# Even and odd output rows, contiguous activation sums, one-bank tiles in the last pass and later fills in an attention-plus-FFN kernel

## The chip, the cores and the metric

One core of one Trainium2 chip. A time is the device time of one execution in microseconds (us); "span" is the time from the first to the last instruction in a profiled execution.

The profiles name the engines PE (TensorE matmuls), PEld (TensorE weight loads), DVE (VectorE), ACT (ScalarE), POOL (GpSimd) and SP (SyncE, which here issues most of the stores). A tile is a piece of memory that the program reserves and guards with waits; a bank is a piece of PSUM, the memory in which TensorE sums its products. A timeline merges instructions of one kind that follow each other into one line.

## The reference

```python
scores = where(mask, scale * q @ k.T, -1e9)      # (8, 8, 576, 64); heads 0-3: the last 32 positions,
attn   = softmax(scores) @ v                     # heads 4-7: positions with the same remainder mod 32
x   = attn.transpose(0, 2, 1, 3).reshape(4608, 512)
out = ((x @ w_a) * (x @ w_b)) @ w_out            # d_ff 1536, out (4608, 512) float32
```

The 4608 tokens are worked off in nine tiles of 512. Attention for later batches runs beside the FFN of earlier ones. In tiles 0 to 2 the product with `w_out` is a plain one; in tiles 3 to 8 ("fast tiles") it is a Strassen-like form with seven products over halves of the tokens, of d_ff and of d_model. Tile 8 is the last pass, in which nothing is left to run beside it.

## The kernel before

The parts that the change and the argument touch. `pf` holds `a * b`, transposed; `ps` holds five sums of its quarters; `wf` holds sums of quarters of `w_out`, `wo_sb` is `w_out` itself. `q` is one of two groups of 128 tokens, `i` a half of the tokens, `g` one of six slices of d_ff.

```python
    FG, HT, HN = FD // 2, TTOK // 2, d_model // 2          # 6, 256, 256
    # a_sb * ab[1] -> pf: token half i are alternate blocks of 16 rows
    halves = lambda x: x.rearrange("p (a i s) -> p a i s", i=2, s=16)
    nc.vector.tensor_mul(pf[:, f, :].rearrange("p (i a s) -> p a i s", i=2, s=16), halves(a_sb), halves(ab[1]))
    ...
    def fast_s(t, n, gs):                                  # the activation sums, on VectorE
        pss[t] = nat.tile([128, 5 * FD * TTOK // 4], ...).rearrange("p (g m) -> p g m", g=FG)
        s = pss[t][:, gs]                                  # g outermost, the five sums side by side in it
        ...
            nc.vector.tensor_tensor(s[:, :, HT:3 * HT]..., x[:, :, 0], x[:, :, 1], op=ALU.add)      # n == 1: sums 1 and 2
    ...
    # weights of the products: 128 neighbouring columns
    full   = lambda e, i: (lambda g, q: pf[:, 2 * g + e, HT * i + 128 * q:HT * i + 128 * (q + 1)])
    summed = lambda n: (lambda g, q: s[:, g, HT * n + 128 * q:HT * n + 128 * (q + 1)])
    ...
    def y_store(eng, t, y, i, q, n=slice(0, d_model)):     # 128 rows of the output
        rows = out[TTOK * t:TTOK * (t + 1), n].rearrange("(q a i s) c -> a s i q c", q=2, i=2, s=16)
        eng.dma_start(out=rows[:, :, i, q], in_=y[i][:, q, n])
    def store_half(i):                                     # fast tiles but the last
        for q in range(2):
            y_store(nc.sync, t, y, i, q)
    ...
    # y_tail, the last pass: for q in 0, 1: products 3 4 1 2 5 6 7 into banks a b c b a c d
        if q == 0:
            bank = {x: mm_bank([128, HN]) for x in "abcd"}
        else:
            o = psum4["o"].tile([128, 2, 512], F32, tag="o", name="end")
            st = pst.tile([128, 2, 512], F32, tag="st", name="end")
            bank = {"a": o[:, 0, :HN], "b": o[:, 1, :HN], "c": st[:, 0, :HN], "d": st[:, 1, :HN]}
    ...
    do(18, fill_v, vl_buf[1])                              # GpSimd: ones beside the values of batch 3
    do(19, fill_v, vs_buf[1])
```

The softmax here doesn't subtract the row's maximum and nothing guards it: scores larger than these inputs give would overflow.

## Time and profile before

| | before |
|---|---|
| time, median of 3 (range) | 337.25 us (336.41 to 339.04) |
| span of the profiled run, mean granted clock | 335.3 us, 0.998 |
| last pass: its first matmul to the end of the last VectorE operation | 318.83 to 330.67, 11.84 us |
| from there to the last byte stored | 2.55 us |
| last byte to the end of the span | 2.07 us |

### The profile page before, as it was taken

Reading aid. Unit: us, or ns where it says so; the run is one execution under the profiler, and the core shown is the slowest. Engines: PE = TensorE matmul, PEld = TensorE weight load, DVE = VectorE, ACT = ScalarE, POOL = GpSimd, SP = SyncE. Lnnn points to the kernel's source line nnn. Section 1 sums busy time; section 2 is a strip of 40 time slices with the busy share of each in tenths; the row PEclk is TensorE's granted clock in tenths of the full one; section 3 lists DMA queues with packets and bytes.
Section 4 is the critical chain, followed back from the end, with each engine's and each line's share of the span. In section 5 each row is a group of like instructions: output and inputs, shape, how many; then the busy total and the mean of one; then the engine's idle time right before and its main releaser. Section 6 shows DMA issues by size and latency. Waiting matters only on the chain.

```text
span 335.3 us, 7662 instructions
## 1 busy us (share of the span) xinstructions
PE 326.2 (97%) x2814; PEld 201.8 (60%) x2814; DVE 254.7 (76%) x489; ACT 202.8 (60%) x329; POOL 173.4 (52%) x295
## 2 busy tenths in 40 slices
PE   8999999999999999999999999999999999999992
PEld 6654555455555555556999885568556844674472
DVE  5867566768878985799999999999877845738641
ACT  5663955468678865776587757875788533223320
POOL 8945836499956644765577457754312031312011
PEclk9999999999999999999999999999999999999999
DMA  9999999599999599969888998899123021003013
GB/s 155 148 203 196 201 181 188 120 191 70 131 221 155 86 99 158 129 116 92 69 83 139 179 98 75 142 164 107 25 62 119 2 73 54 1 12 116 0 29 98
DMA packets 102173, 37.60 MB, mean 112 GB/s; under 512 B 77432, under 2 KB 97784, under 8 KB 102136
## 3 DMA queue, kind: packets, MB, share of 16 engines
q0 software_dynamic: 87760, 19.58, 64.4%
q1 hardware_dynamic: 14104, 17.34, 17.7%
q8 instruction: 22, 0.36, 0.4%
q10 hardware_dynamic: 272, 0.20, 0.2%
q14 instruction: 15, 0.12, 0.1%
HBM read 39.71 MB, written 9.44 MB: 147 GB/s over the span
## 4 chain that ended last, share of the span: by engine, by line
PE 75%; DMA 12%; POOL 7%; DVE 2%; issue 2%; ACT 0%; DVEq 0%; POOLq 0%
PE mm L545 44%; PE mm L650 14%; PE mm L730 7%; DMA vl<-in_v_dram 4%; PE o L454 4%; PE st L356 3%; DMA shared<-in_k_dram 3%; DMA wa_sb<-in_moe_w_a_dram 3%; PE end L678 1%; PE mm L678 1%; POOL shared L195 1%; DMA kl<-in_k_dram 1%; POOL ql L210 1%; DMA natk<-in_k_dram 1%; POOL vl L222 1%
## 5 line engine op out<-in xcount | busy, mean ns | idle before, releaser
L545 PE MATMUL mm<-xT,wb_sb 128*128 128x512 bf16 (+1 forms) x472 | 110.2, 357 | 0.1
L545 PE MATMUL mm<-xT,wa_sb 128*128 128x512 bf16 (+1 forms) x472 | 110.3, 358 | 0.0
L562 ACT COPY a_sb<-mm 128x512 f32<-128x512 f32 x106 | 62.2, 587 | 48.7 <-PE mm L545 46.4
L545 PEld LDWEIGHTS <-wb_sb 128*128 128x128 bf16 x480 | 46.4, 98 | 44.5 <-issue 0.6
L880 POOL CAST pace<-pf 1x1 f32<-1x1 bf16 x84 | 28.4, 339 | 85.1 <-DVE pf L565 73.8
L565 DVE TENSOR_TENSOR pf<-a_sb,mm 128x512 bf16<-128x512 f32 x72 | 48.5, 674 | 17.2 <-PE mm L545 13.8
L545 PEld LDWEIGHTS <-wa_sb 128*128 128x128 bf16 x480 | 42.6, 98 | 31.2
L364 ACT ACTIVATE p<-st 128x576 bf16<-128x576 f32 (+1 forms) x64 | 41.7, 651 | 9.5 <-PE st L356 9.0
L463 ACT ACTIVATE xr<-o 64x576 f32<-64x576 f32 x48 | 31.1, 648 | 26.1 <-PE o L454 25.9
L730 PE MATMUL mm<-wo_sb,pf 128*128 128x512 bf16 x144 | 34.4, 379 | 0.5 <-DMA wo_sb<-in_moe_w_out_dram 0.5
L464 ACT ACTIVATE xr<-xr 64x576 f32<-64x576 f32 x48 | 32.9, 685 | 1.5
L650 PEld LDWEIGHTS <-ps 128*128 128x128 bf16 x300 | 28.5, 98 | 4.4 <-DVE ps L578 1.2
L567 DVE TENSOR_TENSOR pf<-a_sb,mm 128x512 bf16<-128x512 f32 x34 | 23.0, 678 | 8.4 <-ACT a_sb L562 5.9
L470 DVE TENSOR_TENSOR xT<-o,xr 64x288 bf16<-64x288 f32 x48 | 21.5, 448 | 10.4 <-ACT xr L464 9.7
L468 DVE TENSOR_TENSOR xT<-o,xr 64x288 bf16<-64x288 f32 x48 | 21.5, 447 | 8.9 <-ACT xr L464 8.3
L374 DVE TENSOR_TENSOR p<-p,mask_l 128x576 int16<-128x576 int16 x32 | 19.8, 618 | 6.8 <-ACT p L364 6.7
L650 PE MATMUL mm<-wf,ps 128*128 128x256 bf16 x180 | 22.7, 273 | 0.1
L234 POOL DMA_DIRECT2D vs<-in_v_dram x24 | 19.7, 821 | 4.1 <-PE st L356 2.8
L730 PEld LDWEIGHTS <-pf 128*128 128x128 bf16 x144 | 12.9, 98 | 13.9 <-issue 0.8
L880 POOL COPY pace<-y_sb 1x1 f32<-1x1 f32 x18 | 3.2, 177 | 34.0 <-ACT y_sb L633 14.8
L210 POOL DMA_DIRECT2D ql<-in_q_dram x24 | 16.0, 666 | 6.2 <-DMA wo_sb<-in_moe_w_out_dram 4.2
L210 POOL DMA_DIRECT2D kl<-in_k_dram x24 | 16.1, 671 | 4.0 <-issue 3.8
(155 smaller groups left out, 493.7 us busy)
## 6 DMA issues: line engine op xcount, KB each, us to landing
out_dram<-y_sb SPq DMA_DIRECT2D x34, 256.0 KB
vl<-in_v_dram POOLq DMA_DIRECT2D x7, 384.0 KB, 7.2
kl<-in_k_dram POOLq DMA_DIRECT2D x24, 72.0 KB, 3.1
ql<-in_q_dram POOLq DMA_DIRECT2D x24, 72.0 KB, 3.2
vs<-in_v_dram POOLq DMA_DIRECT2D x24, 72.0 KB, 3.8
wo_sb<-in_moe_w_out_dram POOLq DMA_DIRECT2D x4, 384.0 KB, 11.2
natk<-in_k_dram POOLq DMA_DIRECT2D x20, 72.0 KB, 3.2
natq<-in_q_dram POOLq DMA_DIRECT2D x20, 72.0 KB, 3.5
```

The lines of the kernel that those rows point to most:

```text
L210: nc.gpsimd.dma_start(out=t[32 * h:32 * h + 32], in_=src[b, h].rearrange("(i y) d -> y i d", y=32))
L364: nc.scalar.activation(p[:M, :, :W], st[:M, :, :W], ACT.Exp, scale=scale)
L463: nc.scalar.activation(r, sums, ACT.Ln)
L464: nc.scalar.activation(r, r, ACT.Exp, scale=-1.0)
L468: nc.vector.tensor_mul(dst[:, W * half:W * (half + 1)], o[:64, j, :W], r[:, j])
L545: nc.tensor.matmul(ps_[:, c0:c0 + n], lhsT=w[:, kk, 128 * f:128 * (f + 1)], rhs=xT[:, kk, x0:x0 + n], start=(kk == first and c0 == 0), sto ...
L562: nc.scalar.copy(a_sb, ab[0])
L565: nc.vector.tensor_mul(pf[:, f, :].rearrange("p (i a s) -> p a i s", i=2, s=16), halves(a_sb), halves(ab[1]))
L567: nc.vector.tensor_mul(pf[:, f, :], a_sb, ab[1])
L650: nc.tensor.matmul(bank[b][:, q], lhsT=lhs(g, q), rhs=rhs(g), start=new and q == 0 and g == 0, stop=g == FG - 1, skip_group_check=True)
L730: nc.tensor.matmul(y, lhsT=pf[:, f, 128 * j:128 * (j + 1)], rhs=wo_sb[:, f], start=(f == 0), stop=(f == FD - 1))
L880: nc.gpsimd.tensor_copy(pace, done)
```

## The change

Its intent: make two output rows that come from one partition neighbours in memory, so that one store of 4 KB runs replaces two of 2 KB runs; store each sum as one contiguous block with a gap behind it; free the last pass from waits for tiles that hold two banks; and take two long fills of ones out of GpSimd's way. The diff, with the line of the old side left out where the new one tells enough:

```diff
+    SW = HT + 16
-                    shared[b] = nat.tile([128, 5 * FD * TTOK // 4], BF16, tag="shared", name="shared")
+                    shared[b] = nat.tile([128, FG * 5 * SW], BF16, tag="shared", name="shared")
 ... fast_s
-            pss[t] = nat.tile([128, 5 * FD * TTOK // 4], ..., name="ps").rearrange("p (g m) -> p g m", g=FG)
-        s = pss[t][:, gs]
+            pss[t] = nat.tile([128, FG * 5 * SW], ..., name="ps").rearrange("p (n g m) -> p n g m", g=FG, n=5)
+        s = pss[t][:, :, gs, :HT]
+            nc.vector.tensor_tensor(s[:, 1:3], x[:, 0], x[:, 1], op=ALU.add)            # n == 1; 0 and 2 alike
 ... products
-        full = lambda e, i: (lambda g, q: pf[:, 2 * g + e, HT * i + 128 * q:HT * i + 128 * (q + 1)])
-        summed = lambda n: (lambda g, q: s[:, g, HT * n + 128 * q:HT * n + 128 * (q + 1)])
+        full = lambda e, i: (lambda g, q: pf[:, 2 * g + e, HT * i + q:HT * (i + 1):2])
+        summed = lambda n: (lambda g, q: s[:, n, g, q:HT:2])
 ... y_store
-        rows = out[TTOK * t:TTOK * (t + 1), n].rearrange("(q a i s) c -> a s i q c", q=2, i=2, s=16)
+        rows = out[TTOK * t:TTOK * (t + 1), n].rearrange("(a i s q) c -> a s i q c", i=2, s=8, q=2)
 ... store_half
-            for q in range(2):
-                y_store(nc.sync, t, y, i, q)
+            rows = out[TTOK * t:TTOK * (t + 1)].rearrange("(a i s q) c -> a s i (q c)", i=2, s=8, q=2)
+            nc.sync.dma_start(out=rows[:, :, i], in_=y[i].rearrange("p q c -> p (q c)"))
 ... y_tail, q == 1
-                bank = {"a": o[:, 0, :HN], "b": o[:, 1, :HN], "c": st[:, 0, :HN], "d": st[:, 1, :HN]}
+                bank = {"a": psum4["o"].tile([128, 2, 512], F32, tag="o", name="end")[:, 0, :HN],
+                        "b": pst.tile([128, 2, 512], F32, tag="st", name="end")[:, 0, :HN],
+                        "c": mm_bank([128, HN]), "d": mm_bank([128, HN])}
 ... schedule
-        do(18, fill_v, vl_buf[1])
-        do(19, fill_v, vs_buf[1])
+        do(27, fill_v, vl_buf[1])
+        do(28, fill_v, vs_buf[1])
```

## The prediction

> **What bounds the kernel now.** I read the page first, then the chain of work that ended last, then the timelines and the waits of TensorE (PE) from 60 us on, then the last 13 us of every engine.
>
> ```profile
> PE 326.2 (97%) x2814; PEld 201.8 (60%) x2814; DVE 254.7 (76%) x489; ACT 202.8 (60%) x329; POOL 173.4 (52%) x295
> PEclk9999999999999999999999999999999999999999
> ```
>
> PE is busy for 97% of the span at an undiminished clock. Busy is not peak, so I looked at the spacing of matmuls in the chain of work. The change touches the six token tiles whose output product is the seven-product form (84 matmuls of 256 columns each instead of 48 of 512); two pieces of the chain are one such tile and the tile before the last pass:
>
> ```profile
> 289.10 9.17 PE mm L650 x84
> 298.27 20.72 PE mm L545 x96
> ```
>
> 9.17 us / 84 = 109.2 ns per 256-column matmul, 20.72 / 96 = 215.8 ns per 512-column one. Nothing waits there. The same spacing holds from 60 us to 323 us, except in a few places. The waits of PE and of its weight loads between 60 us and the end are therefore the whole stock that a change can win without removing matmuls:
>
> ```profile
> PE end L678 <- DVE y_sb L703: 0.6, 1, 0.6
> PE end L678 <- ACT y_sb L693: 0.5, 1, 0.5
> PE end L678 <- ACT ya L683: 0.5, 1, 0.5
> PEld L678 <- issue: 2.0, 3, 0.8
> PEld L650 <- DVE ps L578: 1.2, 4, 0.3
> ```
>
> All three PE waits are in the last pass, where the second half (q=1) of the last tile is computed. The timeline of all engines at that place:
>
> ```profile
> 323.50 0.82 PE L678 MATMUL end<-wf,pf 128*128 128x256 bf16 x6
> ...
> 324.36 0.37 ACT L683 COPY ya<-end 128x256 f32<-128x256 f32 x1 [1.59 <-PE end L678]
> 324.78 0.82 PE L678 MATMUL end<-wf,pf 128*128 128x256 bf16 x6 [0.46 <-ACT ya L683]
> ...
> 327.46 0.81 PE L678 MATMUL end<-wo_sb,ps 128*128 128x256 bf16 x6 [0.46 <-ACT y_sb L693]
> ...
> 329.51 0.49 PE L678 MATMUL end<-wf,ps 128*128 128x128 bf16 x6 [0.58 <-DVE y_sb L703]
> ...
> 330.38 0.29 DVE L706 TENSOR_TENSOR y_sb<-ye,mm 128x128 f32<-128x128 f32 x1
> ```
>
> A group of six should take 6 x 0.109 = 0.655 us. So the second group could have started at 324.16 and started at 324.78 (0.62 us lost); the one that started at 326.18 ended its issue at 326.84, the next came at 327.46 (0.62); the one of 328.11 ended at 328.77, the next came at 329.51 (0.74). The sum, 1.99 us, is the "2.0, 3 times" of the weight loads. The code says why: bank b is the second half of the two-bank tile that holds bank a, d the second half of c's tile, and each stalled group writes one half while ScalarE or VectorE reads the other. Product 4 goes into b and needs nothing of what the copy of a gives. These are waits for a tile, not for data.
>
> Two smaller losses stand at 81 and 91 us:
>
> ```profile
> 74.74 1.41 POOL L110 MEMSET vl<- 128x1536 bf16 x1
> 78.31 1.82 POOL L110 MEMSET vs<- 72x2048 bf16 x1
> ...
> 79.82 0.78 DVE L299 STREAM_TRANSPOSE tk<-kl 128x576 bf16<-128x576 bf16 x1 [0.94 <-DMA kl<-in_k_dram]
> 80.53 0.88 DVE L468 TENSOR_TENSOR xT<-o,xr 64x288 bf16<-64x288 f32 x2
> ...
> 81.46 0.43 PE L454 MATMUL o<-p,vl 128*128 128x96 bf16 x6
> ```
>
> The four 512-column matmuls from 80.38 end their issue at 81.24; the o group comes at 81.46, after DVE's xT read bank o. DVE was late because the transpose in front of it waited for keys that GpSimd (POOL) issued behind a fill of ones. At 91 us the same: six matmuls from 89.97 end at 91.27, the next group comes at 91.44, behind a DVE transpose of natk that had waited 1.31 us. Together 0.22 + 0.17 = 0.39 us.
>
> **What the Trainium skill says.** (1) "TensorE: Matmul & The Clock Gate", section Back-to-back issue gap: warm, N / 2.4 + 2.5 ns, so 109.2 and 215.8 ns. The trace agrees to the tenth: these stretches have no slack to give. (2) The same page, Weight-path perf modes: fast weight load holds for 128 non-fp32 columns "packed or strided", with column steps up to 1,024 elements. The change reads 510 of its weights with a step of 2. No weight in the kernel before has such a step, so its trace can't confirm it. It does show the margin: eight load-and-multiply pairs of 72 columns (L454) pass in 0.26 us, so a packed load takes at most 33 ns of PE's rate, against 109 ns for a 256-column matmul. (3) "PSUM — Partial Sum Buffer", PSUM bank collisions: two engines clash per bank and 32-partition quadrant, and different banks run clean. So the three tail waits aren't needed by the memory; a tile of one bank each should do away with them. (4) "VectorE: DVE Perf Modes", Mode 2x_1P: two results a cycle need 16-bit data with step 1. The sums take 680 ns for 1024 elements, 1193 for 2048: 0.50 ns for each further element, so they are in that mode already. The new layout keeps runs of 256 with step 1, so I expect no gain or loss there.
>
> **The change part by part.**
>
> *Even and odd rows.* Only the 510 weight loads of fast tiles get a step of 2. With a fourfold slowdown, 4 x 33 = 132 ns, they would show; with a twofold one, 66 ns, they stay under 109. By (2) I count 0. The 12 matmuls of 128 columns at the very end (about 55 ns each) have the least cover; a twofold slowdown costs there 12 x 11 = 0.13 us at most. Output rows come in pairs, so one 4 KB run replaces two 2 KB runs: 10 stores fewer on SP. Nothing waits for them; DMA is nearly idle after 268 us. 0.
>
> *Contiguous sums.* Same element counts, same number of instructions. The four stalls of L650 behind L578 remain: in the timeline eight matmuls from 158.01 should be issued by 158.88 and the next comes at 159.09, so about 0.2 us of PE each, set by DVE's queue, not by layout. But the list of the built program shows new waits. With the sum as the outer index, a write of two sums for the last group covers, as an interval, other groups of those sums. In the fast tiles the wait of product 7 moves forward by four matmuls; it is for a subtraction that ends at 158.96, some 0.8 us before it is needed, so 0. In the last pass the first weight load of product 2 now waits for the addition L580:
>
> ```profile
> 320.75 0.41 DVE L580 TENSOR_TENSOR ps<-pf 128x512 bf16<-128x512 bf16 x1
> ```
>
> It ends at 321.16 and PE starts product 2 at 320.88 now, so it would start at about 321.22: a new loss of 0.35 us, on the path.
>
> *One-bank tiles.* a and b get tiles of their own, c and d come from the rotating pool, whose previous readers ended over 1 us earlier. What is left are true needs. With q=1 starting at 323.46 (323.50 + 0.35 - 0.39): product 4 at 324.11, 1 at 324.77, 2 at 325.51 (it accumulates on b and must follow DVE's read; before, 1.40 us from the start of 4), 5 at 326.17, 6 at 326.82, 7 at 327.48 and its second cut at 327.81, issued by 328.14. Now POOL's subtractions count: ScalarE's copy of b ends near 326.74, POOL's two of 0.73 follow and end near 328.23. DVE's last two take 0.29 each from about 328.3 and end at 328.86, against 330.67 now.
>
> *Fills.* POOL loses 1.41 and 1.82 us at 74 to 80 us, so keys and values come up to 3.2 us earlier and the DVE waits of 0.94 and 1.31 us should go, with the 0.39 us of PE. Put behind batch 3's rows, near 87 to 92 us, they wait for no DMA in the built program, and POOL is back at its pace by 94 us, where it idles 1.39 us.
>
> The sum: 330.67 - 328.86 = 1.8 us (made of 1.99 saved in the tail, less 0.18 to POOL's chain and the reuse of b, plus 0.39, less 0.35). The last stores follow the last DVE operation as now, 4.6 us. 337.25 - 1.8 = 335.4 us.
>
> **The rivals.** *Strided loads are slow.* If spacing rose from 109 to 120 ns, 510 matmuls would cost 5.6 us: 341. For it: no trace of a step here. Against: 33 against 109 ns, and the skill's row. *New waits eat the gain.* If product 2 waits longer, or POOL's chain or SP's issues (0.60 us each) take the place of the tile waits, some 0.7 to 1 us is left: 336.4. The built program shows only the one wait, so I think it counted. *Everything outside the tail is hidden.* Then the 0.39 us falls away: 335.8. *Fewer, larger stores relieve the loads.* At 165 to 270 us the DMA queues are used, but PE waits for none of it: 0.
>
> **Range and chances.** The terms that could go missing sum to under 1 us, the three runs before spread over 2.6 us, so I take 333.9 to 337.2. A gain over 2% needs 6.7 us; all PE waits after 60 us do not reach 4. A loss over 2% needs the first rival at its full size. Faster 0.03, within 2% 0.94, slower 0.03.
>
> **What would show it right or wrong.** In the new profile PE's three waits at L678 are gone and the whole last pass from 318.83 to DVE's end takes about 10.4 us, not 11.8. L650 stays at 84 in 9.17 us, weight loads at about 98 ns mean. One new wait near 0.3 us stands before product 2. The DVE waits for kl and natk at 79 and 89 us are gone, the fills stand near 87 to 92 us. In the page's list of issues the 34 stores of 256 KB become 14, with 10 of 512 KB. I am wrong if L650's spacing grows, if PE waits on another bank in the last pass, or if the time falls by over 3 us: then something outside PE's waits was binding.

## More of the kernel before

"Last byte stored" is the end of the latest record of the two hardware DMA queues in the trace.

The medians and ranges are over all runs of a kernel; three groups hold one slow run: after_oldsums (351.03), rot_only (342.05) and the 11 runs of before that it is measured against (341.59).

## The result, and the profile after

| | before (same rounds) | after |
|---|---|---|
| time, median (range), 6 runs each | 337.37 (336.41 to 339.04) | 333.50 (333.10 to 336.53) |
| ratio, 95% interval | 1 | 0.9894 (0.985 to 0.9938) |
| span, clock of the profiled run | 335.3, 0.998 | 331.4, 1.0 |

A ratio is the mean of one kernel's fast runs over the mean of the other's fast runs of the same rounds, so it isn't quite the ratio of the medians. "Within 2%" was right; the time lies 0.4 us below the predicted range, and the gain is 3.9 us by the medians where 1.8 us was predicted.

First the head of each page. The span line of the kernel before, then span and busy shares of the changed kernel (its granted clock is in the table above):

```profile
span 335.3 us, 7662 instructions
```

```profile
span 331.4 us, 7611 instructions
...
PE 323.1 (98%) x2781; PEld 201.8 (61%) x2814; DVE 255.0 (77%) x489; ACT 202.6 (61%) x329; POOL 172.8 (52%) x295
```

The weight loads (PEld) take 201.8 us as before, so a step of 2 costs them nothing. The 2781 matmuls against 2814 loads are lost records, not lost work: at the places of the lost ones the starts of two neighbours lie 432 ns apart where 216 ns is the rule. The changed kernel's chain of work has the same fast tile as the one shown of before:

```profile
288.06 9.17 PE mm L650 x84
```

84 matmuls in 9.17 us again. Next the timeline of TensorE in the last pass (start, duration, line, tiles, count, and in brackets the idle time before and what ended it), with VectorE's last operation:

```profile
317.78 1.47 PE L678 MATMUL mm<-wf,pf 128*128 128x256 bf16 x12
319.09 0.82 PE L678 MATMUL mm<-wf,ps 128*128 128x256 bf16 x6
320.18 1.48 PE L678 MATMUL mm<-wo_sb,ps 128*128 128x256 bf16 x12 [0.27 <-DVE ps L581]
321.50 1.47 PE L678 MATMUL mm<-wf,ps 128*128 128x256 bf16 x12
322.81 1.47 PE L678 MATMUL end<-wf,pf 128*128 128x256 bf16 x12
324.12 0.82 PE L678 MATMUL mm<-wf,ps 128*128 128x256 bf16 x6
324.87 1.47 PE L678 MATMUL end<-wo_sb,ps 128*128 128x256 bf16 x12
326.17 1.49 PE L678 MATMUL mm<-wf,ps 128*128 128x256 bf16 x18
...
327.62 0.49 DVE L706 TENSOR_TENSOR y_sb<-ye,mm 128x128 f32<-128x128 f32 x2
```

The three waits for `end` are gone; one new wait stands before product 2 at 320.18. The waits of TensorE and of its loads from 60 us to the end name it (line: us in all, times, longest):

```profile
PE mm L678 <- DVE ps L581: 0.3, 1, 0.3
...
PEld L650 <- DVE ps L579: 1.2, 4, 0.3
...
PEld L678 <- DVE ps L581: 0.5, 1, 0.5
```

Now the sum over the span. Each row is a difference of two times read from the traces:

| stretch | before | after | gain |
|---|---|---|---|
| start of span to start of last pass | 318.83 | 317.78 | 1.05 |
| last pass (to the end of the last VectorE operation) | 11.84 | 10.32 | 1.52 |
| last VectorE operation to last byte stored | 2.55 | 1.99 | 0.56 |
| last byte to end of span | 2.07 | 1.27 | 0.80 |
| sum | 335.28 | 331.36 | 3.92 |

The prediction had the second row and 0.39 us of the first. The last two rows, 1.36 us, it had put at zero. Of the first row 0.77 us arise before 60 us, where TensorE waits for the output weights `wo_sb`, and 0.28 us at 80 to 91 us, where of the 0.39 us of stalls 0.10 are left.

### The profile page after: what moved, and what is told of

Its sections match the earlier page's. It is cut to its first block, busy times and chain, and to the rows that moved or that the text cites. A ratio compares the mean times of both kernels' runs of the same rounds, so it can differ in the third digit from the quotient of the medians.

```text
span 331.4 us, 7611 instructions
## 1 busy us (share of the span) xinstructions
PE 323.1 (98%) x2781; PEld 201.8 (61%) x2814; DVE 255.0 (77%) x489; ACT 202.6 (61%) x329; POOL 172.8 (52%) x295
## 4 chain that ended last, share of the span: by engine, by line
PE 81%; DMA 13%; POOL 2%; DVE 1%; issue 1%; ACT 1%; POOLq 0%; SPq 0%; DVEq 0%
PE mm L546 49%; PE mm L650 14%; PE mm L730 7%; DMA vl<-in_v_dram 4%; PE o L455 4%; PE st L357 4%; DMA shared<-in_k_dram 3%; DMA wa_sb<-in_moe_w_a_dram 3%; PE mm L678 1%; DMA raw<-in_q_dram 1%; DMA natk<-in_k_dram 1%; PE end L678 1%; POOL wa_sb L244 0%; POOL wb_sb L244 0%; DVE tk L300 0%
## 5 line engine op out<-in xcount | busy, mean ns | idle before, releaser
L546 PE MATMUL mm<-xT,wa_sb 128*128 128x512 bf16 (+1 forms) x453 | 108.8, 357 | 0.9
L546 PE MATMUL mm<-xT,wb_sb 128*128 128x512 bf16 (+1 forms) x463 | 108.5, 357 | 0.3
L730 PE MATMUL mm<-wo_sb,pf 128*128 128x512 bf16 x140 | 33.6, 379 | 0.3
L880 POOL COPY pace<-y_sb 1x1 f32<-1x1 f32 x18 | 3.1, 175 | 33.2 <-ACT y_sb L633 14.9
```

The costliest lines, as they stand in the source:

```text
L546: nc.tensor.matmul(ps_[:, c0:c0 + n], lhsT=w[:, kk, 128 * f:128 * (f + 1)], rhs=xT[:, kk, x0:x0 + n], start=(kk == first and c0 == 0), sto ...
L730: nc.tensor.matmul(y, lhsT=pf[:, f, 128 * j:128 * (j + 1)], rhs=wo_sb[:, f], start=(f == 0), stop=(f == FD - 1))
L880: nc.gpsimd.tensor_copy(pace, done)
```

## The experiments

All kernels gave the correct result. For each I read the same stretches as above; the table at the end of this section collects them.

### The parts alone

`banks_only` is the kernel before with the edit of `y_tail` alone; `fills_only` with the two schedule lines alone; `rows16` keeps the old rows and one store per `q` but cuts rows into sixteen outer blocks; `after_rows8` is the changed kernel with eight outer blocks in place of sixteen.

```diff
 # rows16, against before (tensor_mul and y_store)
-  halves ... s=16 ; "(q a i s) c -> a s i q c", q=2, i=2, s=16
+  halves ... s=8  ; "(q a i s) c -> a s i q c", q=2, i=2, s=8
 # after_rows8, against after (tensor_mul, y_store and store_half)
-  halves ... s=16 ; "(a i s q) c -> ...", i=2, s=8, q=2
+  halves ... s=32 ; "(a i s q) c -> ...", i=2, s=16, q=2
```

> The kernel before with nothing but the one-bank tiles in the last pass. My theory: the three PE waits of 0.62, 0.62 and 0.74 us before the groups of the second half go; there is no new wait before product 2, since the sums keep their old layout; GpSimd's two subtractions take back about 0.1 us. So the last VectorE operation ends about 1.9 us earlier in the last pass and the time is 0.994 to 0.995 of before; the stretch from the last VectorE operation to the end of the span stays near 4.6 us. Rival (the stores or GpSimd's subtractions take the place of the waits): the PE waits go and less than 1 us is gained. Rival (the shorter end of the span in the changed kernel also comes from the one-bank tiles): that stretch shrinks to about 3.3 us and the ratio is near 0.990.

> The kernel before with nothing but the fills of ones moved behind batch 3's rows. My theory: PE loses 0.1 us less at 81 us and 0.17 us less at 91 us, nothing else changes, ratio 0.999. The PE wait for wo_sb near 47 us (0.63 us in the trace of before, none in the trace of the changed kernel) lies ahead of the fills and can't be moved by them: it is there or not by chance of the loads. Rival (the 0.77 us by which the changed kernel is ahead at 56 us belong to the change): they come back in only one of the four kernels of this call, or in those that share a part.

> The kernel before with rows still in two blocks per tile (no even and odd rows, no strided weights, same sums), but with the output's outermost dimension of 16 blocks of 8 rows instead of 8 blocks of 16. My theory: the last stores are cut over 16 DMA engines instead of 8, so the stretch from the last VectorE operation to the end of the span falls from 4.6 to about 3.3 us and the ratio is 0.996; the three PE waits of the last pass stay. Rival (the shorter end comes from the pairs of adjacent rows): the stretch stays at 4.6 us, ratio 1.0.

> The changed kernel with even and odd rows kept, but the output's outermost dimension of 8 blocks of 16 row pairs instead of 16 blocks of 8. My theory: the last stores are back on 8 DMA engines, the stretch from the last VectorE operation to the end is about 4.6 us instead of 3.3, and the ratio to before is 0.992 to 0.994 where the changed kernel had 0.989. Rival (pairs of adjacent rows make the stores fast): the stretch stays at 3.3 us and the ratio at 0.989.

Measured against 337.22 us (7 runs of before): banks_only 336.15, ratio 0.9985 (0.9953 to 1.0017); fills_only 336.06, 0.9975 (0.9948 to 1.0002); rows16 336.07, 0.9975 (0.9948 to 1.0003); after_rows8 335.29, 0.9955 (0.9928 to 0.9982).

Of the expected ratios that of banks_only (0.994 to 0.995) lies outside its interval. Those of fills_only (0.999) and after_rows8 (0.992 to 0.994) are off the middle values but inside the intervals; that of rows16 (0.996) is met. rows16 came to 3.84 us from the last VectorE operation to the end where 3.3 us were expected, since only the stores got faster.

banks_only takes all three waits away and its last pass falls from 11.84 to 9.97 us, but by the ratio the time falls by 0.15% only. The interval, from 0.5% faster to 0.2% slower, holds no gain at all as well as the 1.3 us by which the profiled spans differ (335.3 and 334.0). The time from the last VectorE operation to the last byte grew from 2.55 to 3.17 us, and at 81 us it drew a stall of 0.51 us. Why the stores take longer is seen in the busy share of the 16 DMA engines, in tenths, in 40 slices of 321 to 336 us. Before, banks_only, after_rows8, after, rows16, in this order:

```profile
DMA  0000100000553355545434504454445400000000
```

```profile
DMA  0010000001733454555454455555100000000000
```

```profile
DMA  0001000000065335555555345555520000000000
```

```profile
DMA  2000000079998100184868940000000000000000
```

```profile
DMA  0100000029999500000840295817600000000000
```

With eight outer blocks a store keeps half of the 16 engines busy (digits about 5) and the stores follow each other without a break; with sixteen it fills them (9) and they are apart. The page "DMA: Bandwidth & Descriptors" of the Trainium skill, section Why a DMA increments its semaphore by 16 and not by 1, says that a transfer is spread over the largest number up to 16 that divides the outermost dimension of both sides. The trace agrees in a second place: the queue of ScalarE, q10, carries two stores of 128 pieces in the whole program; with 8 or 16 more packets per store, one for each engine, that makes 2 x 136 = 272 or 2 x 144 = 288. From section 3 of the pages before and after:

```profile
q10 hardware_dynamic: 272, 0.20, 0.2%
```

```profile
q10 hardware_dynamic: 288, 0.20, 0.2%
```

The issue of a store is shorter too, and so it is in rows16 (537/587/627 and 561/606/650 ns), which has the old rows. The group of the line of `y_store`, before and after (min/median/max ns):

```profile
L605 SPq DMA_DIRECT2D out_dram<-y_sb x25: 603/604/1657, 180.2 to 330.7; - x25
...
L605 ACTq DMA_DIRECT2D out_dram<-y_sb x2: 619/919/1219, 328.7 to 330.4; - x2
```

```profile
L605 SPq DMA_DIRECT2D out_dram<-y_sb x5: 537/537/557, 322.9 to 328.2; - x5
...
L605 ACTq DMA_DIRECT2D out_dram<-y_sb x2: 560/610/659, 326.8 to 327.9; - x2
```

From the last VectorE operation to the last byte, by pace of the last pass and number of blocks:

| | 8 blocks | 16 blocks |
|---|---|---|
| last pass slow (11.84 us) | before 2.55 and 2.75, fills_only 2.30, rot_only 2.67 | rows16 1.75 |
| last pass fast (9.97 or 10.32 us) | banks_only 3.17, after_rows8 3.61 | after 1.99, 1.95, 1.98; three_parts 2.00 |

So one-bank tiles and sixteen blocks are worth more together than apart. A last pass that is 1.5 to 1.9 us shorter produces the same stores in less time, and with eight blocks it gives back 0.6 to 1.1 us of that against the 2.55 us of before (2.30 to 2.75 us in four traces). In these two stretches banks_only gains 1.25 us, rows16 0.80 us and three_parts, which has both, 2.43 us. Why after_rows8 needs 0.4 us more than banks_only for its stores is not located. after_rows8 shows the size in the changed kernel: from the last VectorE operation to the last byte it needs 1.6 us more, and its time loses 1.8 us against the 333.5 of the result.

fills_only removes both stalls (0.00 left at 81 and at 91 us). Their size is not fixed: a second trace of the kernel before, below, has 0.95 us at 91 us alone. Over all traces but that of after_oldsums, the stalls between 80 and 92 us are 0.42 us on average in the five without the later fills (0.00 to 1.06) and 0.05 us in the eleven with them (0.00 to 0.28), and the last pass starts at 318.62 and at 318.23 us. Both differences are near 0.39 us, but they are small against the spread of the single traces.

### The changed kernel again, with the old sums, without the gap, and three parts without the rows

```diff
 # after_oldsums, against after: the layout of the sums as before the change
-  .rearrange("p (n g m) -> p n g m", g=FG, n=5) ; summed: s[:, n, g, q:HT:2]
+  .rearrange("p (g m) -> p g m", g=FG)          ; summed: s[:, g, HT * n + q:HT * (n + 1):2]
 # after_pad0, against after
-    SW = HT + 16
+    SW = HT
 # three_parts: before, with the edits of banks_only, fills_only and rows16
```

> The changed kernel once more, for a second trace. What is tested is whether the PE wait for wo_sb near 47 us belongs to the change. It was 0.00 us in the first trace of the changed kernel, and 0.47 to 0.79 us in five others (before, and four kernels with parts of the change). My theory: it is luck of the loads, and a second trace of the changed kernel has some 0.5 us of it, so the span is about 332 us. Rival (the change removes it): it is 0 again. Everything from 60 us on should repeat: the last pass 10.3 us from its first matmul to the last VectorE operation, 2.0 us from there to the last byte stored, 1.3 us from that to the end of the span.

> The changed kernel with the sums back in their old layout (group outside, sum inside), weights still read with a step of 2. My theory: the PE wait of 0.34 us before product 2 of the last pass goes, and the last pass takes 10.0 us instead of 10.3; the spacing of the 256-column matmuls stays at 109 ns; the ratio is 0.001 below that of the changed kernel. Rival (contiguous sums pay somewhere else, in the strided weight loads or in VectorE's sums): 84 matmuls of a fast tile take longer than 9.2 us, or the sums take longer than 680 and 1193 ns.

> The changed kernel without the 16 columns of padding behind each sum. My theory: the padding buys nothing, all durations and the last pass are the same within 0.1 us. Rival: weight loads with a step of 2 or VectorE's sums get slower without it. It is also a further trace for the wait for wo_sb.

> The kernel before with one-bank tiles in the last pass, the fills moved, and the output's outermost dimension of 16 blocks, but without even and odd rows, without strided weights, with the old sums and all 10 stores of before. My theory: the last pass takes 10.0 us (no new wait), the last byte is stored 1.8 to 2.0 us after the last VectorE operation as in the changed kernel, so these two stretches together are 0.3 us shorter than in the changed kernel. From the last byte to the end of the span it stays at 2.1 us as in all kernels that keep the 10 stores (the changed kernel has 1.3), so the ratio to before is 0.991 to 0.993. Rival (the pairs of rows themselves make the last stores fast): the stretch to the last byte is 3 us or more, as with one-bank tiles alone.

Measured against 337.12 us (8 runs of before): after_again 333.70, 0.9901 (0.9871 to 0.993); after_oldsums 347.42, 1.0256 (1.0208 to 1.0303); after_pad0 333.68 (one run, unknown state); three_parts 333.73, 0.9899 (0.987 to 0.9927).

The gap of 16 columns is worth nothing here. The layout of the sums is worth nothing by itself either, as far as these intervals tell (three_parts has the old one), but with stepped weight loads it is needed: the three fast runs of after_oldsums have a mean of 346.7 us against 333.9 of after_again, a loss of 12.8 us. My expectation, which had after_oldsums 0.1% ahead of the changed kernel, failed. The waits of TensorE and of its loads from 60 us on, in after_oldsums, and its timeline of TensorE in the first fast tile:

```profile
PE mm L651 <- DVE ps L581: 9.4, 5, 2.4
...
PEld L651 <- DVE ps L581: 10.4, 5, 2.6
```

```profile
157.28 0.70 PE L651 MATMUL mm<-wf,ps 128*128 128x256 bf16 x3
160.39 0.72 PE L651 MATMUL mm<-wf,ps 128*128 128x256 bf16 x5 [2.41 <-DVE ps L581]
161.37 3.40 PE L651 MATMUL mm<-wf,ps 128*128 128x256 bf16 x16
```

Three matmuls of product 1 go, the fourth waits until the addition for sums 1 and 2 is done. Product 1 reads sum 0 only. In the list of the built program that weight load reads elements 3840 to 4094 in steps of 2, and the addition writes 2816 to 3327, 4096 to 4607, 5376 to 5887 and 6656 to 7167: no element in common, but the load lies between the first and the last. With contiguous loads (three_parts, before) the same pair has no wait. So the wait was put in when the program was built, for a load with a step, and isn't one of the data. With each sum contiguous the addition lies wholly outside what product 1 reads.

Such a wait can cost more than its own length. In the windows view of after_oldsums (stretch, then length, busy time of each engine with its count, granted clock, DMA share, GB/s), the first three lines are of the first fast tile, the last two follow the waits of the third and the fourth:

```profile
157.00:161.00 4.00, 1.56 (x17) 1.00 (x14) 3.93 (x6) 0.65 (x1) 2.65 (x4) 1.00 1.13 121
161.00:164.60 3.60, 3.60 (x25) 2.71 (x24) 1.56 (x4) 1.33 (x2) 0.00 (x0) 0.53 0.44 36
164.60:168.00 3.40, 3.40 (x39) 3.07 (x37) 1.23 (x3) 1.78 (x3) 0.80 (x2) 1.00 0.00 0
...
237.40:241.00 3.60, 3.60 (x40) 3.26 (x39) 1.68 (x4) 1.33 (x2) 0.00 (x0) 1.00 0.58 52
...
273.60:277.00 3.40, 3.40 (x23) 2.55 (x23) 0.88 (x2) 1.33 (x2) 0.00 (x0) 0.51 0.00 0
```

After 2.6 us of waiting the granted clock is 0.53 for 3.6 us, so by my estimate 3.6 x 0.47 = 1.7 us more are lost. Over the five tiles, first to last matmul, after_oldsums takes 14.29, 14.01, 12.64, 13.69 and 9.61 us and after_again 10.06 four times and 9.06: 14.9 us, of which 10.4 are the waits. The remaining 4.5 us fit the lowered clock, but they aren't spread evenly. The weight loads of the five tiles waited 2.6, 2.6, 2.6, 2.0 and 0.6 us; beyond its wait a tile lost 1.6, 1.4, 0.0, 1.6 and 0.0 us against after_again. After the wait of the third tile, as long as that of the first, the clock stayed at 1.00; after the shorter one of the fourth it fell to 0.51. What decides between them these runs don't show. The Trainium skill, "TensorE: Matmul & The Clock Gate", section Why this matters for your kernels, advises no idle gaps above about 3 us; here the clock fell after three of four waits of 2.0 to 2.6 us.

three_parts shows no wait before product 2: its last pass takes 9.96 us against 10.32 in the changed kernel. The new wait is thus worth 0.36 us and comes from the contiguous sums.

### The last byte to the end

All kernels with the stores of before take 2.05 to 2.19 us from the last byte to the end, the changed ones 1.25 to 1.28. At the end SyncE goes through waits for the semaphores of the eight hardware DMA lanes in a fixed order; transfers take the lanes in turn. In before the last store is on the second lane, with ten stores fewer it is on the eighth. The starts of these waits in us after the last byte, from the traces' instruction records:

| lane waited for | 1 | 2 | 3 | 4 | 5 | 6 | 7 | 8 |
|---|---|---|---|---|---|---|---|---|
| before | 0.10 | 0.34 | 0.41 | 0.47 | 0.53 | 0.59 | 0.65 | 0.71 |
| after | -1.25 | -1.18 | -1.12 | -1.06 | -0.91 | -0.12 | 0.06 | 0.36 |

In both, the last store is known to be done at 0.34 to 0.36 us. Before, six more waits of 0.06 us follow, 0.37 us in all. A second difference is a pause on GpSimd among the closing drains. The groups of the closing lines (count, ns, first and last start), before and after:

```profile
L907 POOLq DRAIN  x3: 106/198/1669, 328.7 to 334.9; - x3
...
L907 POOLq EVENT_SEMAPHORE_RANGE_CLEAR  x1: 139/139/139, 334.4 to 334.4; - x1
```

```profile
L907 POOLq DRAIN  x3: 51/106/1702, 326.8 to 331.1; - x3
...
L907 POOLq EVENT_SEMAPHORE_RANGE_CLEAR  x1: 139/139/139, 330.9 to 330.9; - x1
```

From the end of the clearing instruction to the start of the last drain it is 0.32 us before and 0.03 after, and that drain takes 0.20 us before and 0.05 after. The pause always stands before the 453rd recorded instruction of GpSimd; the changed kernel has only 451 there, since four waits fell away. Four more runs:

```diff
 # rot_only: before, with two pairs of stores of tile 0 merged, two transfers fewer (three_rot: three_parts likewise)
-        nc.sync.dma_start(out=out[r0:r0 + 128], in_=y_sb)
+        if t > 0:
+            nc.sync.dma_start(out=out[r0:r0 + 128], in_=y_sb)
+        elif j % 2 == 1:
+            nc.sync.dma_start(out=out[r0 - 128:r0 + 128].rearrange("(j p) c -> p j c", p=128), in_=yst[t])
 # after_split2: after, with the two stores of tile 3 split by q, two transfers more
+            if t == 3:
+                for q in range(2):
+                    y_store(nc.sync, t, y, i, q)
+                return
 # before_again: no edit
```

A first form, which merged the two stores of a fast tile on the old rows, did not build: the pattern needs four dimensions and a transfer takes three. That is what even and odd rows are for.

> The kernel before with one edit: the four output stores of the first tile (256 rows each pair) are merged into two, so two hardware-queue transfers fewer run, early, around 50 us. The last store of the program then signals the eighth of the eight DMA semaphores that the closing waits go through in order, instead of the second. Theory (the closing waits cost time by their order): from the last stored byte to the end of the span 1.25 to 1.35 us instead of 2.07; the time about 0.6 to 0.8 us less, ratio near 0.998. Rival (the shorter end of the changed kernel comes from its layout of rows or from ten stores fewer): 2.05 to 2.1 us from last byte to end, ratio 1.000.

> One-bank tiles, the later fills and the split into sixteen blocks, on the rows and sums of the kernel before (the three parts of an earlier run), plus the same merging of two pairs of stores of the first tile. Theory: last byte to end 1.27 us instead of 2.09, no new wait before product 2 in the last pass (worth 0.34 us against the changed kernel), so it comes out 0.3 us ahead of the changed kernel: span 331.0 to 331.7 us, ratio to before 0.987 to 0.990. Rival (the even and odd rows with contiguous sums are worth something that the three parts lack): stays 0.5 us or more behind the changed kernel, ratio above 0.9905.

> The changed kernel with the two stores of one tile (about 180 us) split in two each, so two transfers more, and the last store signals the second of the eight semaphores again, as before the change. Theory: last byte to end 2.07 us instead of 1.27; the whole 0.8 us of the end is lost, ratio to before near 0.9915 to 0.993. Rival (only the seven remaining waits of 0.06 us each depend on the order; the late drain on GpSimd, 0.35 us, has another cause): 1.70 us from last byte to end. Second rival (layout): 1.27 us, ratio 0.990.

> The kernel before, once more, for a second trace: whether the wait of TensorE for the output weights near 47 us (0.63 us in its first trace; 0.00, 0.43 and 0.35 in three traces with the changed kernel's program) is a property of the program or a draw. If of the program: 0.6 to 0.9. If a draw: as likely under 0.5. Last pass 11.84 us, from the last VectorE operation to the last byte 2.5 us, from there to the end 2.07 us.

Measured against 337.70 us (11 runs): rot_only 336.12, 0.9955 (0.9924 to 0.9986); three_rot 333.37, 0.9879 (0.9855 to 0.9904); after_split2 334.37, 0.9908 (0.988 to 0.9935); before_again 337.58 (one run).

From the last byte to the end: rot_only 1.67, three_rot 1.56, after_split2 1.64, before_again 2.19. My expectation of 1.25 to 1.35 for rot_only and three_rot was too low, and that of 2.07 for after_split2 too high: the order of the lanes alone is worth about 0.4 us, and the pause goes its own way. In rot_only and three_rot it still stands, before the 453rd instruction, though that is now the clearing instruction and not the drain; in after_split2, with 452 instructions, there is none.

before_again settles the early part. The wait for `wo_sb` (waits of TensorE, 20 to 60 us) is listed for before, not for before_again; for after_again and after_third, not for after. The lines of before, after_again and after_third:

```profile
PE mm L730 <- DMA wo_sb<-in_moe_w_out_dram: 0.5, 1, 0.5
```

```profile
PE mm L730 <- DMA wo_sb<-in_moe_w_out_dram: 0.3, 1, 0.3
```

```profile
PE mm L730 <- DMA wo_sb<-in_moe_w_out_dram: 0.9, 1, 0.9
```

By the starts of the matmuls TensorE loses 0.63 and 0.23 us there in two traces of before, and 0.00, 0.43 and 1.09 us in three of the changed kernel. It is a draw, so the 0.77 us of the first pair of traces is not to be put down to the change. before_again also shows the stall that the fills cause, at a size three times that of the first trace (timelines of VectorE and TensorE):

```profile
90.07 0.71 DVE L304 STREAM_TRANSPOSE tk<-natk 128x512 bf16<-128x512 bf16 x1 [2.09 <-DMA qz10l<-tq]
```

```profile
91.72 0.42 PE L454 MATMUL o<-p,vs 72*128 72x72 bf16 x8 [0.79 <-DVE xT L470]
```

### The pause on GpSimd, and a last comparison

```diff
 # after_pool5: after, five one-element fills more on GpSimd at about 92 us
         do(28, fill_v, vs_buf[1])
+        for _ in range(5):
+            do(28, nc.gpsimd.memset, vs_buf[1][:1, 0, 0, D:D + 1], 1.0)
 # after_third: after, unedited.  three_rot_b: three_rot, unedited.
```

> The changed kernel with five one-element fills of ones added on GpSimd right behind the moved fills, at about 40 us, far from the end; one wait falls away beside them, so GpSimd's stream is four instructions longer (455 recorded instead of 451), as long as that of the kernel before. In all traces so far a pause of 0.32 us stood before the 453rd recorded GpSimd instruction wherever the stream reached it (in the closing drains), and none where it ended sooner. Theory (the pause belongs to that position in the stream): the pause is back, last byte to end 1.58 us instead of 1.27, with the order of the DMA semaphores unchanged. Rival (it belongs to something else in the kernels before): 1.27 us.

> The changed kernel, unedited, beside the next run on one chip, so that the two can be compared without the scatter from call to call. Both theories: ratio to before 0.989 to 0.990, last byte to end 1.27 us, last pass 10.32 us.

> The kernel with three parts of the change and two pairs of early stores merged, once more, beside the changed kernel. Theory (rows and sums are worth nothing by themselves; the last pass is 0.35 us shorter without contiguous sums, the end 0.3 us longer by the pause on GpSimd): within 0.3 us of the changed kernel, ratio to before 0.988 to 0.990. Rival (even and odd rows bring something of their own): 0.7 us or more behind the changed kernel.

Measured against 337.60 us (11 runs): after_pool5 333.76 (one run, unknown state); after_third 333.61, 0.9873 (0.983 to 0.9916); three_rot_b 333.37, 0.9886 (0.9832 to 0.9939).

In after_pool5 the pause is back, before the 453rd instruction, 0.32 us long, though the added fills lie some 240 us earlier. (In the trace they run from 91.8 to 92.5 us, behind the moved fills; the "about 40 us" of my expectation was wrong.) Its groups of the closing lines show it as those of before do (clearing at 331.1, last drain at 331.6):

```profile
L909 POOLq DRAIN  x3: 106/198/1702, 327.1 to 331.6; - x3
...
L909 POOLq EVENT_SEMAPHORE_RANGE_CLEAR  x1: 139/139/139, 331.1 to 331.1; - x1
```

Last byte to end, by both causes:

| | last store on the second lane | on the eighth lane |
|---|---|---|
| 453 or more GpSimd instructions (pause) | before 2.07, 2.19; three_parts 2.09 | rot_only 1.67; three_rot 1.56, 1.56; after_pool5 1.71 |
| fewer (no pause) | after_split2 1.64 | after 1.27, 1.26, 1.28 |

The two are worth about 0.4 us each and add up to the 0.80. That the position decides is shown; what happens there is not. three_rot_b and after_third can't be told apart (0.2 us by the medians, intervals that overlap widely). So no gain of rows and contiguous sums shows beyond the two changes of the end that ten stores fewer and four GpSimd waits fewer bring; three_rot reaches the same time without them. A difference of a few tenths of a us these intervals can't exclude.

| | time | span | last pass | to last byte | to end | stalls at 80 to 91 us |
|---|---|---|---|---|---|---|
| before | 337.37 | 335.3 | 11.84 | 2.55 | 2.07 | 0.39 |
| banks_only | 336.15 | 334.0 | 9.97 | 3.17 | 2.15 | 0.5 |
| fills_only | 336.06 | 334.2 | 11.84 | 2.30 | 2.05 | 0 |
| rows16 | 336.07 | 334.0 | 11.84 | 1.75 | 2.09 | 0.2 |
| three_parts | 333.73 | 332.6 | 9.96 | 2.00 | 2.09 | 0 |
| three_rot | 333.37 | 331.8 | 9.97 | 2.00 | 1.56 | 0 |
| after_rows8 | 335.29 | 334.0 | 10.32 | 3.61 | 1.25 | 0.15 |
| after | 333.50 | 331.4 | 10.32 | 1.99 | 1.27 | 0.10 |

## Why the prediction was wrong, point by point

- **Tail waits.** Right. 1.99 less 0.18 us were predicted for the one-bank tiles; the last pass lost 1.87 us (11.84 to 9.97 in banks_only, where nothing else changed).
- **The new wait before product 2.** Right: 0.35 us predicted, 0.36 us measured (10.32 in the changed kernel, 9.96 in three_parts).
- **Fills.** Right in kind. 0.39 us were predicted from one trace; 0.29 us of them went in the first trace after, and in fills_only all. The mean over all traces, 0.42 against 0.05 us, agrees with it, by luck in part, since single traces have from 0.00 to 1.06 us. fills_only alone gained 0.25% (0.8 us), but its interval reaches zero. One sign failed: of the two DVE waits that should be gone, the one for natk is, the one for kl is not (0.9 us before, 0.8 in the changed kernel, 0.2 to 1.0 in eight other traces with later fills, none in fills_only and after_rows8).
- **Stepped loads, sums on VectorE.** Right: 84 matmuls in 9.17 us before and after, loads at 201.8 us in both, the sums of 1024 elements 680 ns in both. The rival of slow loads is refuted. (The page gives the formula of point (1) for a single isolated matmul; that it holds for a stream of loads and matmuls too is what the trace shows.) I missed why the sums were made contiguous: with the old layout the stepped loads carry false waits (after_oldsums, 346.7 us in its fast runs).
- **Ten stores fewer: 0.** Wrong. They shift the last store from the second to the eighth lane, about 0.4 us at the end.
- **"The last stores follow the last DVE operation as now, 4.6 us."** This is the step that failed. The 4.6 us became 3.26. I took them for a constant and never split them. They hold 2.55 us of transfers, set by how many DMA engines a store uses and how tightly the stores follow each other, and 2.07 us of closing waits, set by the lane of the last store and by the length of GpSimd's stream. The change touched all four. Split over sixteen blocks, the stores went to 1.99 us; left at eight, they went to 3.61 (after_rows8), 1.06 us more than the prediction took. after_rows8 took 335.29 us, next to the predicted 335.4, by luck: its slower stores nearly cancel the 0.8 us that its closing waits win. The error of 1.36 us is most of the miss: with it added, the changed kernel would have taken 334.9 us.
- **What would prove it wrong** held: "if the time falls by over 3 us: then something outside PE's waits was binding." It did, by 3.9 us, and what was binding besides PE's waits was the stretch behind the last VectorE operation, stores and closing waits.

With 1.52 us in the last pass, about 0.4 for the fills, 0.56 and 0.80 behind the last pass, 3.3 us are accounted for. The medians differ by 3.9 and the ratio by 1.06% (3.6 us, with an interval from 2.1 to 5.1). The rest, if there is one, lies within the scatter of the kernel before (336.2 to 338.6 us in ten fast runs of one chip) and is not located.

## What to carry to other kernels

Before a tail is called constant, split it: last compute to last byte, last byte to end, and ask of each store how many DMA engines its outermost dimension allows. A shorter tail needs stores that keep up: taken alone, the removal of 1.9 us of waits gave back 0.6 us behind the last pass, where half-spread stores followed each other without a break, and the gain in time wasn't clear of noise. When an operand gets a step, look at the waits of the built program as well as at the speed of the load; false waits of 2.0 to 2.6 us on TensorE cost 1.4 to 1.6 us more than their length in three cases of four, since the clock fell after them.

## What the Trainium skill lacked or had wrong

- "DMA: Bandwidth & Descriptors", the rule for the number of engines: right (8 blocks against 16), but it gives no price. Here a store's issue on SyncE took 603 ns with eight and 537 ns with sixteen, the longer of two on ScalarE 1219 against 659 ns, and the last byte came 3.61 against 1.99 us after the last VectorE operation.
- No page has the closing waits: the eight DMA lanes are waited for in a fixed order, 0.06 us each, so a last store on the second lane costs about 0.4 us more than on the eighth.
- No page that I found tells of a pause tied to the 453rd GpSimd instruction: 0.32 us in every trace whose stream reached it, none in the others. "Runtime: NRT & Kernel Launch", section Instruction fetch mechanics, describes instructions fetched in blocks; no run here shows that this is it.
- "TensorE: Matmul & The Clock Gate": the advice to keep gaps under about 3 us is too wide here; a wait of 2.6 us was followed by a granted clock of 0.53 for 3.6 us and one of 2.0 us by 0.51 for 3.4 us, though another of 2.6 us left it at 1.00. What its section Weight-path perf modes says, that fast weight load reads packed or strided columns, agrees with the trace (98 ns per load and 201.8 us of loads in both kernels).
- "PSUM — Partial Sum Buffer": nothing wrong, but it doesn't say that two banks in one tile make the program wait (1.99 us here) though the banks don't collide.
